# Decay rows of an attention tile: two transfers of 64 partitions in place of one with two source rows

## The chip, the cores and the metric

The kernel runs on one core of a Trainium2 chip. The metric is the device time of one execution in microseconds. A core has five engines with instruction streams of their own: PE (matrix multiply), DVE (vector), ACT (scalar, activation functions), POOL (general purpose) and SP, which here only issues transfers. Transfers are carried out by 16 DMA engines. Each engine runs its own stream in order and waits at semaphores for the others.

## The reference, cut to what matters

Three layers follow one another: a linear attention with decay, an MLP with x times cos(x), and a gated MLP. The change touches the attention.

```python
# x: (4, 8, 768, 32), a: (4, 8, 768), B and C: (4, 8, 768, 16); chunk = 32
for c in range(nc):
    la = log_a[:, :, sl]
    cum = np.cumsum(la, axis=-1)
    L = np.exp(cum[:, :, :, None] - cum[:, :, None, :]) * causal
    M = np.einsum('bhin,bhjn->bhij', Cc, Bc) * L
    y_intra = np.einsum('bhij,bhjd->bhid', M, xc)
    y_inter = np.einsum('bhin,bhnd->bhid', Cc, state) * np.exp(cum)[..., None]
    y[:, :, sl] = y_intra + y_inter
    Bx = np.einsum('bhjn,bhjd->bhjnd', Bc, xc) * decay_from_j[..., None, None]
    state = decay_full[..., None, None] * state + np.sum(Bx, axis=2)
x = y.transpose(0, 2, 1, 3).reshape(3072, 256)
h = x @ w_in                          # 256 -> 2048
x = (h * np.cos(h)) @ w_out           # 2048 -> 256
out = (sigmoid(x @ w_gate) * (x @ w_val)) @ w_out2   # 256 -> 1536 -> 256
```

## The kernel before

The 768 positions are cut into six blocks of 128 (`j`), and each block holds the four batches (`b`), so that a block of one batch is an attention tile: 128 tokens, eight heads. For `j` = 0 the tile is computed as one chunk of 128 (`add_att_first`). For `j` = 1 to 5 (`add_att`) it is two chunks of 64 tokens, and chunks and heads are laid over the partitions: partitions 0 to 63 hold one half of the heads, 64 to 127 the other.

The products of decays inside a chunk are made by one scan on the DVE (line 762): it runs over 512 columns (two chunks, four heads, 64 tokens) and writes the tile `lt`. Every partition needs the decays of all 64 tokens of its half of the heads, so the 512 values of a half are repeated over 64 partitions. This is the spread (`add_spread`, line 573): a transfer from `a_chunk`, a copy of the decays in DRAM, to a tile `ab` of 128 x 512 float32. There are three `ab` tiles in turn, and 20 spreads, one for each tile of blocks 1 to 5. Two products with `lt` follow: `bd` (line 765), which PE turns into the state's gain, and `g` (line 800), from which PE makes the tokens' output.

Beside the spread, `add_loads` (line 542) issues for every block: B and C (tile `bc`, 64 KB for each batch, 64-byte pieces), x (`xs`, 128 KB for each batch), two transfers that exchange the halves of x (`xw`), four that halve B (`bh`), and one for the decays of the state (`an`, from `a_clip`). The weights of the MLPs come as float64 words into slots of the tile `x2` (lines 354 and 359 for the first layer, 467 for the second), and ACT and DVE unpack them (lines 371 to 387): the step `three` on ACT (line 377) reads each load first. All transfers are issued by SP, in one order.

No order of instructions is written by hand. `Order.add` notes each step with its cost in nanoseconds for each engine that could do it, what it reads and what it writes. `Order.rank` gives it a due time, counted back from those who need it, and `Order.run` simulates the engines and always takes the step that can begin first, the more urgent one of two. For a step on SP the cost is the time that the transfer takes of a DMA pipe that all share, and `Issues(cost, n)` says that the step issues `n` transfers: SP is then held for 620 ns times `n`, or until the pipe has come to within 1100 ns of the transfer's end. A changed cost or number thus moves steps on every engine. MLP steps of the first layer begin as soon as the first block's attention and the first weights are there, and the planner interleaves them with the attention of later blocks.

Of the kernel before, what the change touches and what calls it, by code (L numbers as in the profile page):

```python
# [67 lines left out]
class Order:  # L68
# [17 lines left out]
    def add(self, where, fn, r=(), w=(), tag=None, turn=None):  # L86
        op = Op()
        op.engs, op.fn, op.tag, op.turn = dict(where), fn, tag, turn
        op.users, op.ready = [], {e: 0.0 for e in op.engs}
        deps = set()  # L90
        for x in r:
            if x in self.last_w:
                deps.add(self.last_w[x])
        for x in w:
            if x in self.last_w:
                deps.add(self.last_w[x])
            deps.update(self.reads.get(x, ()))
        i = len(self.ops)
        for x in r:
            self.reads.setdefault(x, []).append(i)  # L100
        for x in w:
            self.last_w[x] = i
            self.reads[x] = []
        op.left = len(deps)
        for d in deps:
            self.ops[d].users.append(i)
        self.ops.append(op)
# [111 lines left out]
def linear_attention__then__cos_mlp__then__gated_mlp_kernel(  # L219
# [23 lines left out]
    nc = tc.nc  # L243
    NB, H, S, D = x.shape
# [11 lines left out]
    add = order.add  # L256
# [8 lines left out]
    def ring(pool_, n, shape, dt, name):  # L265
        return [pool_.tile(shape, dt, name=f"{name}{i}") for i in range(n)]
# [37 lines left out]
    TC = T // 2  # L304
    a_chunk = dram.tile([NB, 2, 2 * NJ, 4, TC], F32, name="a_chunk")
# [4 lines left out]
    ab_t = ring(att_p, 3, [128, H * TC], F32, "ab")  # L310
# [231 lines left out]
    def add_loads(j):  # L542
        i = j % NL
        t = slice(j * T, (j + 1) * T)
        for b in range(NB):
            for src, dst, room, cost in ((C, bc_t[i][:, 1, b], ("bc", i, 1, b), 704), (B, bc_t[i][:, 0, b], ("bc", i, 0, b), 704),
                                         (x, x_whole(i, b), ("xs", i, b), 832)):
                add({"SP": cost}, lambda e, src=src, dst=dst, b=b: nc.sync.dma_start(  # L548
                    out=dst, in_=src[b, :, t, :].rearrange("h t n -> t h n")), w=[room])
        if j == 0:  # L550
            return

        def turn_x(e):
            for half in range(2):
                nc.sync.dma_start(
                    out=xw_t[i][HALF[half]],
                    in_=xs_t[i][HALF[1 - half]].rearrange("t (b g d) -> t b g d", b=NB, g=2)[:, :, half])

        def halve_b(e):
            for half in range(2):  # L560
                for c in range(2):
                    nc.sync.dma_start(  # L562
                        out=bh_t[i][HALF[half], c],
                        in_=bc_t[i][HALF[c], 0].rearrange("t b (g k) n -> t b g (k n)", g=2)[:, :, half])

        add({"SP": Issues(960, 2)}, turn_x, r=[("xs", i, b) for b in range(NB)], w=[("xw", i)])
        add({"SP": Issues(1536, 4)}, halve_b, r=[("bc", i, 0, b) for b in range(NB)], w=[("bh", i)])
        add({"SP": 800}, lambda e: nc.sync.dma_start(
            out=an_t[i].rearrange("p b t -> p (b t)"),
            in_=a_clip[:, j].rearrange("h b t -> h (b t)")[:, None].to_broadcast([H, N, NB * T])),  # L570
            r=[("a_clip", b) for b in range(NB)], w=[("an", i)])

    def add_spread(j, b):
        u = (j * NB + b) % 3
        add({"SP": 800}, lambda e: nc.sync.dma_start(
            out=ab_t[u],
            in_=a_chunk[b, :, 2 * j:2 * j + 2].rearrange("g c k t -> g (c k t)")[:, None].to_broadcast([2, TC, H * TC])),
            r=[("a_chunk", k) for k in range(4)], w=[("ab", u)] + (["a_f", "a_part", "a_res", "sel_b"] if u == 2 else []))

    def x_whole(i, b):  # L580
        return xs_t[i].rearrange("t (b h d) -> t b h d", b=NB, h=H)[:, b]

    HALF = (slice(0, 64), slice(64, 128))
# [510 lines left out]
    def open_later(e):  # L1094
# [18 lines left out]
        out=mask_sb[:, 0:64], in0=mask_sb[:, 0:64], in1=mask_sb[:, 64:128], op=ALU.add), w=["mask"])  # L1113
    add({"DVE": dve2(2)}, lambda e: nc.vector.tensor_copy(out=pair_sb, in_=mask_sb[:, 0:64:32]), r=["mask"], w=["pair"])
    for i in range(1, 4):
        add({"DVE": dve2(128), "POOL": pool(128)},
            lambda e, i=i: engine[e].tensor_copy(out=id4[:, i], in_=id_sb), r=["id"], w=["id4"])
    add_clip()
    add_loads(0)
    for b in range(NB):  # L1120
        add_att_first(b)
    add({"POOL": pool(512)}, lambda e: nc.gpsimd.tensor_tensor(
        out=id8, in0=id_sb[:, None, 0:TC].to_broadcast([128, H, TC]),
# [8 lines left out]
    for s, step in enumerate(steps):  # L1132
        j, f = step[:2]
        if j and f == 0:
            add_loads(j)
            for b in range(NB):
                add_spread(j, b)
                add_att(j, b)
        add_mlp1(s)
# [54 lines left out]
```

## Time and profile before

| | |
|---|---|
| median of 3 runs | 677.08 us (677.05 to 677.61) |
| the profiled execution | 676.78 us |
| its span, first to last instruction | 674.6 us |
| PE busy | 616.0 us (91%) |
| DVE, ACT, POOL busy | 509.2, 392.7, 195.0 us |
| mean granted PE clock | 0.971 of full speed |
| moved by transfers | 40.80 MB in 118552 packets |

The span is what the trace shows; 2.2 us of the profiled execution lie around it. Times in the trace count from the start of the span. Busy time tells how long an engine worked, not whether anybody waited for it; for that there are the waits (an instruction's idle time before it, and who ended it) and the chain that ended last.

### The profile page before, as it was taken

To read this page: it belongs to the slowest core of one execution; us is meant where nothing else is said; L and a number is where in the kernel's file an instruction comes from. 1 tells how busy PE (TensorE), PEld (TensorE's weight loads), DVE (VectorE), ACT (ScalarE), POOL (GpSimd) and SP (SyncE) were. 2 spreads that over 40 slices of the span, in tenths; PEclk is the share of its full clock that TensorE was granted. 3 is DMA by queue.
4 is the path that set the end of the run, shared out by engine and by line. 5 is a ranking of instruction groups with operands and counts; after the bars stand their busy time and mean duration, and the time that the engine had idled before them with its cause. 6 is when DMAs were issued, how large, how long until landed. Compare 5 with 4: busy or idle time off the path is not lost.

```text
span 674.6 us, 11328 instructions
## 1 busy us (share of the span) xinstructions
PE 616.0 (91%) x4260; PEld 490.7 (73%) x4260; DVE 509.2 (75%) x902; ACT 392.7 (58%) x672; POOL 195.0 (29%) x165
## 2 busy tenths in 40 slices
PE   4665696999969899999999999999999999999997
PEld 2343375787757678778678877888878888888886
DVE  7845684899847885886668889999997778775565
ACT  2324476876646567567578985776653346444442
POOL 2100234565325334335446743232100002010000
PEclk9995987999989999999999999999999999999999
DMA  6874749424352430000022122130002100021001
GB/s 121 131 189 112 148 81 206 94 60 82 76 137 67 123 83 1 28 7 1 2 64 78 48 63 63 62 95 0 1 5 35 26 0 1 1 35 29 1 1 62
DMA packets 118552, 40.80 MB, mean 60 GB/s; under 512 B 100387, under 2 KB 105539, under 8 KB 118499
## 3 DMA queue, kind: packets, MB, share of 16 engines
q1 hardware_dynamic: 118499, 40.09, 26.3%
q8 instruction: 33, 0.54, 0.4%
q14 instruction: 20, 0.16, 0.1%
HBM read 32.54 MB, written 4.92 MB: 56 GB/s over the span
## 4 chain that ended last, share of the span: by engine, by line
PE 73%; DMA 9%; SPq 7%; DVE 6%; ACT 2%; issue 2%; ACTq 0%; DVEq 0%
PE bank L328 62%; PE two_banks L328 10%; DMA x<-in_moe_w_out_dram 5%; SPq L548 4%; DMA ab<-a_chunk 2%; DMA bc<-in_C_dram 1%; DVE bank L1050 1%; SPq L562 1%; DVE gm L858 1%; SPq L354 1%; ACT gm L856 1%; DVE lt L762 1%; PE two_banks L747 0%; ACT gh L335 0%; DVE gm L854 0%
## 5 line engine op out<-in xcount | busy, mean ns | idle before, releaser
L340 POOL TENSOR_TENSOR gl<-gm,gh 128x512 fp32r<-128x512 f32 x104 | 148.3, 1429 | 315.2 <-ACT gh L335 200.3
L328 PE MATMUL bank<-xt_hi,w 128*128 128x512 f32 x573 | 161.5, 402 | 6.1 <-DVE gm L858 5.1
L328 PEld LDWEIGHTS bank<-xt_hi,w 128*128 128x128 f32 x573 | 108.5, 193 | 29.7 <-DVE gm L858 5.5
L1050 DVE TENSOR_TENSOR bank<-bank,cp 128x512 f32<-128x512 f32 x144 | 96.2, 694 | 43.4 <-PE bank L328 38.6
L328 PE MATMUL bank<-gh,w 128*128 128x512 f32 x408 | 116.0, 404 | 11.5 <-ACT gh L335 11.5
L335 ACT ACTIVATE gh<-gm 128x512 fp32r<-128x512 f32 x140 | 87.0, 627 | 60.7 <-DVE gm L1078 40.2
L328 PE MATMUL bank<-xt_lo,w 128*128 128x512 f32 x354 | 105.2, 395 | 0.0
L328 PEld LDWEIGHTS bank<-gh,w 128*128 128x128 f32 x408 | 78.2, 195 | 28.6 <-ACT gh L335 12.6
L858 DVE TENSOR_TENSOR gm<-gm,bank 128x512 f32<-128x512 f32 x96 | 65.2, 681 | 37.1 <-ACT gm L856 37.1
L852 ACT ACTIVATE gm<-bank,quarter_sb 128x512 int32<-128x512 f32 x96 | 65.2, 681 | 28.6 <-PE bank L328 22.4
L854 DVE TENSOR_TENSOR gm<-gm,bank 128x512 f32<-128x512 int32 x96 | 65.3, 682 | 21.9 <-ACT gm L852 21.2
L856 ACT ACTIVATE gm<-gm,right_sb 128x512 f32<-128x512 f32 x96 | 68.7, 718 | 19.2 <-DVE gm L854 18.3
L328 PEld LDWEIGHTS bank<-xt_lo,w 128*128 128x128 f32 x354 | 67.1, 191 | 14.1
L328 PE MATMUL bank<-gl,w 128*128 128x512 f32 x204 | 67.3, 405 | 0.2 <-POOL gl L340 0.2
L1075 ACT ACTIVATE gm<-bank 128x512 f32<-128x512 f32 x72 | 42.5, 599 | 41.7 <-DVE bank L1050 25.8
L335 ACT ACTIVATE cp<-bank 128x512 f32<-128x512 f32 x72 | 42.5, 597 | 29.0 <-PE bank L328 27.2
L1078 DVE TENSOR_TENSOR gm<-gm,bank 128x512 f32<-128x512 f32 x72 | 47.2, 681 | 2.2 <-PE bank L328 1.9
L328 PEld LDWEIGHTS bank<-gl,w 128*128 128x128 f32 x204 | 38.7, 195 | 8.5 <-POOL gl L340 0.6
L328 PE MATMUL bank<-xt_hi,own 128*128 128x512 f32 x135 | 37.7, 393 | 1.0 <-DVE bank L1050 1.0
L328 PE MATMUL bank<-op,w 128*128 128x512 f32 x126 | 34.9, 390 | 0.0
L328 PE MATMUL bank<-xt_lo,own 128*128 128x512 f32 x126 | 34.6, 390 | 0.2 <-ACT gm L1075 0.2
L340 DVE TENSOR_TENSOR gl<-gm,gh 128x512 fp32r<-128x512 f32 x46 | 31.2, 688 | 2.2 <-PE two_banks L328 1.4
(163 smaller groups left out, 838.4 us busy)
## 6 DMA issues: line engine op xcount, KB each, us to landing
x<-in_moe_w_out_dram SPq DMA_DIRECT2D x12, 512.0 KB
ab<-a_chunk SPq DMA_DIRECT2D x20, 256.0 KB
xs<-in_x_dram SPq DMA_DIRECT2D x24, 128.0 KB
x<-in_moe_w_in_dram SPq DMA_DIRECT2D x6, 512.0 KB
x<-in_moe_w_gate_dram SPq DMA_DIRECT2D x6, 512.0 KB
x<-in_moe_w_val_dram SPq DMA_DIRECT2D x6, 512.0 KB
out_dram<-x SPq DMA_DIRECT2D x128, 16.0 KB
bc<-in_C_dram SPq DMA_DIRECT2D x24, 64.0 KB
```

The source lines that it names most:

```text
L328: nc.tensor.matmul(out_, lhsT, rhs, start=start, stop=stop, skip_group_check=True)
L335: nc.scalar.activation(out=out_, in_=in_, func=ACTF.Copy)
L340: engine[eng].tensor_tensor(out=out_, in0=in0, in1=in1, op=ALU.subtract)
L354: nc.sync.dma_start(out=raw()[:, 0:256 * m].rearrange("p (k f) -> p k f", k=KD), in_=w_in[:, cols].rearrange("(k p) f -> p k f", p=128))
L548: add({"SP": cost}, lambda e, src=src, dst=dst, b=b: nc.sync.dma_start(out=dst, in_=src[b, :, t, :].rearrange("h t n -> t h n")), w=[room])
L852: add({"ACT": act_b(512) - 40}, lambda e: nc.scalar.activation(out=ri, in_=hp, func=ACTF.Identity, bias=quarter_sb), r=hr + ["round"], w=[ ...
L854: add({"DVE": dve(512)}, lambda e: nc.vector.tensor_tensor(out=g, in0=ri, in1=hp, op=ALU.subtract), r=hr, w=[("gm", u)])
L856: add({"ACT": act_b(512)}, lambda e: nc.scalar.activation(out=g, in_=g, func=ACTF.Sin, scale=-TURN, bias=right_sb), w=[("gm", u)])
L858: add({"DVE": dve(512)}, lambda e: nc.vector.tensor_tensor(out=g, in0=g, in1=hp, op=ALU.mult), r=hr, w=[("gm", u)])
L1050: add({"DVE": dve(512)}, lambda e: nc.vector.tensor_tensor(out=bank[to], in0=bank[x], in1=later["cp"][i], op=ALU.add), r=bank_r[x][:1] + [ ...
L1075: add({"ACT": act(512)}, lambda e, i=i, bk=bk: nc.scalar.activation(out=g_of("gm", i), in_=bank[bk], func=ACTF.Sigmoid), r=bank_r[bk][:1] ...
L1078: add({"DVE": dve(512)}, lambda e, i=i, bk=bk: nc.vector.tensor_tensor(out=g_of("gm", i), in0=g_of("gm", i), in1=bank[bk], op=ALU.mult), r ...
```

## The change

`add_spread` issues two transfers, one for each half of the partitions: 64 partitions, each of which reads the same 512 values. Before, one transfer went over 128 partitions, with a source of two rows, each repeated 64 times. The planner's cost of a spread stays 800 ns in all, and it is told that the step has two issues. The cost that the planner has for the transfer `an` is 1600 instead of 800 ns; that transfer itself is as it was.

```diff
@@ -565,16 +565,21 @@
-        add({"SP": 800}, lambda e: nc.sync.dma_start(
+        add({"SP": 1600}, lambda e: nc.sync.dma_start(
             out=an_t[i].rearrange("p b t -> p (b t)"),
             in_=a_clip[:, j].rearrange("h b t -> h (b t)")[:, None].to_broadcast([H, N, NB * T])),
             r=[("a_clip", b) for b in range(NB)], w=[("an", i)])
 
     def add_spread(j, b):
         u = (j * NB + b) % 3
-        add({"SP": 800}, lambda e: nc.sync.dma_start(
-            out=ab_t[u],
-            in_=a_chunk[b, :, 2 * j:2 * j + 2].rearrange("g c k t -> g (c k t)")[:, None].to_broadcast([2, TC, H * TC])),
+
+        def spread(e):
+            for half in range(2):
+                nc.sync.dma_start(
+                    out=ab_t[u][HALF[half]],
+                    in_=a_chunk[b, half, 2 * j:2 * j + 2].rearrange("c k t -> (c k t)")[None].to_broadcast([TC, H * TC]))
+
+        add({"SP": Issues(800, 2)}, spread,
             r=[("a_chunk", k) for k in range(4)], w=[("ab", u)] + (["a_f", "a_part", "a_res", "sel_b"] if u == 2 else []))
```

On SP, in the loads of block 2 (`bc_103`, `xs_101`) while block 1 is computed, the difference of the orders is this; `x_81` is the tile with the weights' slots, the numbers at the ends of names are those of buffers:

```order
 L548 DMA bc_103<-in_B_dram 128x8x16 x4
-L548 DMA xs_101<-in_x_dram 128x8x32 x4
-L575 DMA ab_107<-a_chunk 128x1x512
+L548 DMA xs_101<-in_x_dram 128x8x32 x3
 L354 DMA x_81<-in_moe_w_in_dram 128x2x256
 L359 DMA x_81<-in_moe_w_out_dram 128x2x256
+L548 DMA xs_101<-in_x_dram 128x8x32
+L578 DMA ab_107<-a_chunk 64x512 x2
 L562 DMA bh_115<-bc_103 64x4x64 x4
```

One pair of weight loads goes ahead of the last x load and of the spread of block 1's last tile.

On SP again, at the spreads of block 2's second and third tile and the loads of block 3 (`bc_104`, `xs_102`):

```order
+L578 DMA ab_105<-a_chunk 64x512 x2
 L548 DMA bc_103<-in_C_dram 128x8x16
-L575 DMA ab_106<-a_chunk 128x1x512
+L578 DMA ab_106<-a_chunk 64x512 x2
+L354 DMA x_81<-in_moe_w_in_dram 128x2x256
+L359 DMA x_81<-in_moe_w_out_dram 128x2x256
 L548 DMA bc_103<-in_C_dram 128x8x16 x2
 L548 DMA bc_104<-in_B_dram 128x8x16 x4
+L548 DMA xs_102<-in_x_dram 128x8x32 x4
+L562 DMA bh_116<-bc_104 64x4x64 x4
 L354 DMA x_81<-in_moe_w_in_dram 128x2x256
 L359 DMA x_81<-in_moe_w_out_dram 128x2x256
```

The pair that came after two C loads and four B loads comes before them, right behind the spread, and the next pair takes its place.

## Rows read from the trace of the kernel before

**Rows 1.** The page, busy us (share of the span) xinstructions of the PE.

```profile
PE 616.0 (91%) x4260; PEld 490.7 (73%) x4260; DVE 509.2 (75%) x902; ACT 392.7 (58%) x672; POOL 195.0 (29%) x165
```

**Rows 2.** Busy time by stretch; the first line names the columns.

```profile
core 0: us, PE busy (x) PEld busy (x) DVE busy (x) ACT busy (x) POOL busy (x), PEclk, DMA share, GB/s
0.00:26.00 26.00, 14.20 (x112) 8.30 (x112) 19.50 (x46) 7.83 (x19) 5.12 (x10) 1.00 0.77 130
...
26.00:127.00 101.00, 69.50 (x583) 49.49 (x576) 64.05 (x106) 52.43 (x86) 24.85 (x18) 0.85 0.70 147
...
100.00:126.00 26.00, 20.34 (x80) 16.18 (x78) 14.19 (x20) 16.76 (x25) 10.74 (x7) 0.87 0.95 185
...
160.00:200.00 40.00, 34.12 (x351) 26.39 (x352) 29.63 (x67) 21.05 (x40) 13.92 (x12) 0.98 0.49 111
```

**Rows 3.** The chain that ended last: start us, us, what.

```profile
38.23 11.87 DMA ab<-a_chunk
...
54.90 10.07 DMA bc<-in_C_dram
...
72.85 10.10 DMA x<-in_moe_w_out_dram
...
185.74 2.67 DMA xs<-in_x_dram
...
189.85 7.08 DMA x<-in_moe_w_out_dram
```

**Rows 4.** Busy time by stretch, columns as above: spreads alone, and xw alone.

```profile
51.00:57.00 6.00, 1.71 (x32) 1.14 (x32) 3.03 (x7) 4.30 (x7) 0.67 (x1) 0.54 0.13 50
...
251.00:252.20 1.20, 1.20 (x7) 1.00 (x6) 1.04 (x3) 1.20 (x4) 0.08 (x1) 1.00 0.84 176
```

**Rows 5.** Issues: KB of each; ns min/median/max of the issue, first and last start.

```profile
ab<-a_chunk SPq DMA_DIRECT2D x20, 256.0 KB
...
L575 SPq DMA_DIRECT2D ab<-a_chunk x20: 488/541/5282, 27.3 to 281.2; - x20
...
L555 SPq DMA_DIRECT2D xw<-xs x10: 590/622/2322, 36.2 to 250.5; - x10
```

**Rows 6.** Instructions of SP in order of time: start us, us, what.

```profile
27.26 0.58 SPq L575 DMA_DIRECT2D ab<-a_chunk  x1
...
49.57 5.28 SPq L575 DMA_DIRECT2D ab<-a_chunk  x1
...
85.38 3.99 SPq L575 DMA_DIRECT2D ab<-a_chunk  x1
```

**Rows 7.** Instructions of PE and ACT: start, us, what [idle before it, who ended it].

```profile
35.49 1.08 PE L328 MATMUL two_banks<-g,xs 128*32 128x128 f32 x16 [2.23 <-DMA xs<-in_x_dram]
...
50.34 0.33 PE L747 MATMUL two_banks<-id_t,bc 128*128 128x128 f32 x1 [3.58 <-DMA bc<-in_C_dram]
...
52.79 0.32 PE L328 MATMUL bank<-xs,bd 64*32 64x64 f32 x2 [2.12 <-DVE bd L765]
...
58.47 0.47 PE L747 MATMUL bank<-id_t,bc 128*128 128x128 f32 x1 [3.97 <-DMA bc<-in_C_dram]
...
65.01 0.47 PE L747 MATMUL two_banks<-id_t,bc 128*128 128x128 f32 x1 [1.24 <-DMA bc<-in_C_dram]
...
83.04 1.19 ACT L377 ACTIVATE x<-x,low_sb 128x1024 int32<-128x1024 uint32 x1 [7.16 <-DMA x<-in_moe_w_out_dram]
...
85.61 2.07 PE L328 MATMUL bank<-xt_hi,w 128*128 128x512 f32 x4 [5.15 <-DVE gm L858]
...
107.71 2.07 PE L328 MATMUL bank<-gh,w 128*128 128x512 f32 x4 [5.66 <-ACT gh L335]
...
199.46 2.08 PE L328 MATMUL bank<-gh,w 128*128 128x512 f32 x4 [5.88 <-ACT gh L335]
```

**Rows 8.** Busy time by stretch, columns as in rows 2: behind that wait.

```profile
198.20:205.00 6.80, 5.54 (x13) 4.39 (x14) 4.58 (x7) 5.39 (x10) 3.82 (x3) 0.50 0.02 6
```

**Rows 9.** Waits of SP's queue from 130 to 420 us: us, times, longest.

```profile
SPq L575 <- DVE lt L762: 31.6, 7, 6.9
```

## Prediction

> **What bounds the kernel now.** The first view is the page's busy times [rows 1]: the PE works for 616.0 of 674.6 us, so 58.6 us of PE idleness is all that a change of transfers can win, apart from clock. The second is the table of stretches [rows 2], to see where that idleness lies. From 26 to 127 us the PE is busy for 69.50 of 101.00 us, and the DMA engines for a share of 0.70. This is the stage in which the first blocks' inputs and the first layer's weights arrive; more than half of the idleness, 31.5 us, is there. The third is the chain that ended last [rows 3]. In this stage it runs through transfers: a spread at 38.23 that took 11.87 us, a C load that took 10.07, a weight load that took 10.10. These are 256 KB, 64 KB and 512 KB; times this long for so little are queueing, so I ask for what.
>
> From 51 to 57 us spreads alone were moving [rows 4]: the DMA share is 0.13 and the rate 50 GB/s. A share of 0.13 of 16 engines is 2.1 engines. So one spread runs on two engines, as many as it has source rows, and its 256 KB (262,144 bytes) [rows 5] take 262/50 = 5.2 us. The other 14 engines are free meanwhile, but not for what comes behind: a transfer that uses all 16 has a piece on each, and lands when its pieces on the two busy ones have had their turn. The SP too is held: at 49.57 and 85.38 us the issue of a spread took 5.28 and 3.99 us instead of a median of 541 ns [rows 5, 6].
>
> Seven of the 20 spreads are issued in the stage, the first at 27.26 and the last at 85.38 us [rows 6]. Its DMA work is 0.70 x 101 = 70.7 us per engine. The spreads are 7 x 5.2 = 36.7 us on two engines, 36.7 x 2/16 = 4.6 as a mean over 16, so everything else is 66.1. If that is evenly laid, the two engines have 66.1 + 36.7 = 102.8 us to do in 101: they are full from end to end, and they set the stage. It fits that the PE's waits there are for what queued behind spreads [rows 7]: x 2.23 us, C 3.58, 3.97 and 1.24, the decay product that follows the scan of a spread 2.12, and 5.15 and 5.66 for MLP results that stand on ACT behind the unpacking of a weight load; at 83.04 us ACT had waited 7.16 us for one [rows 7]. Together that is 24.0 of the 31.5 us.
>
> **The change, part by part.** *The transfer.* Two transfers of 64 partitions and 64 source rows replace one. The nearest row is the pair that turns x (xw, also 64 partitions and 128 KB each): from 251.0 to 252.2 us it ran at 0.84 of 16 engines and 176 GB/s [rows 4]. So I expect each half on all 16. At 176 GB/s a pair takes 262/176 = 1.5 us, which at a share of 0.84 is 1.25 us of each engine. The other end is the spread's own rate on eight times the engines, 5.24/8 = 0.66. Seven cost 4.6 to 8.8 us; I take the middle, 6.7, since nothing here shows 16 engines reading one row. The two full engines come down from 102.8 to 66.1 + 6.7 = 72.8 us, as all others.
>
> *What the stage then takes.* Queues are never full all the time. The share was 0.77 from 0 to 26 us, where no spread runs, and 0.95 from 100 to 126 us, where the spreads are through [rows 2]. With the middle, 0.86, the stage takes 72.8/0.86 = 84.7 us, 16.3 less. The ends are 70.7/0.95 = 74.4 (26.6 less) and 74.9/0.77 = 97.3 (3.7 less). The compute engines can follow: 69.50 us of PE work and 64.05 of DVE work [rows 2] are 82% and 76% of 84.7. The mean granted clock of the stage is only 0.85 of full speed [rows 2], but I add nothing for it: the stage is set by DMA.
>
> *Later.* From 127 us the PE is nearly full but for 160 to 200 us, where 5.9 us are idle [rows 2]. They are the wait of 5.88 us at 199.46 [rows 7], and the chain gives its reason: an x transfer waited for until 188.4, then a weight load that took 7.08 us [rows 3]. After it the granted clock was 0.50 from 198.20 to 205.00 us, with 5.54 us of PE work in it [rows 8], which at the full clock would be 2.8 shorter. So 0 to 8.7 us are to be had. I take 4.0, a little under half, because here the SP also waits for the scans to free a buffer, 31.6 us in seven waits [rows 9], and these stay.
>
> *The SP.* An issue with 64 partitions took 622 ns (xw), one spread 541 [rows 5]. Two are 0.70 us more each time, 7 x 0.70 = 4.9 us in the stage. What covers this are the two blocked issues, 5.28 + 3.99 - 2 x 0.54 = 8.2 us, that should go. Without that cover the 4.9 us would be lost. The 13 later ones, 9.1 us, lie beside the waits for scans.
>
> *The order.* The planner is told of one more issue per spread and of 1600 instead of 800 ns for the decay transfer an. It answers by pulling weight loads ahead of x loads and of the fourth block's B and C loads. That is to the good for the two longest PE waits (85.61 and 107.71 us), which hang on weights. It costs nothing on its own as long as the staging buffer is free when SP comes to the load; otherwise x, B and C queue behind a waiting SP. No instruction is added on PE, DVE, ACT or POOL. I count it as nothing, inside the stage.
>
> Sum: 16.3 + 4.0 = 20.3 us. The profiled execution took 676.78 us, 0.3 less than the median of the runs, 677.08. So 676.8 - 20.3 = 656.5 us, and 656.8 for the median. The bounds are 26.6 + 8.7 = 35.3 (641.8) and 3.7 + 0 (673.4).
>
> **The rivals.** *A new wait takes the place.* In-order engines find the next late thing: DVE at 76% has little slack, ACT stands behind each unpacking, SP behind a staging buffer. Of the seven PE waits all 24 us would have to shrink; if only those on C and x do (2.23 + 3.58 + 3.97 + 1.24 = 11.0) and half of that comes back as another wait, the gain is 5.5 and the time 672. Chance 0.13.
>
> *The split gives nothing.* The Trainium skill (DMA: Bandwidth & Descriptors, Rules for kernel authors) says of two transfers to disjoint partition halves "Don't bother": both spray over the same 16 engines and serialize. By that rule the 4.9 us of issues are all that changes, which is 682. The rows speak against it here, because the single transfer was on 2.1 engines, not 16 [rows 4]; another section of that page (Why a DMA increments its semaphore by 16 and not by 1) takes the engine count from the outermost sizes of both sides, which would be 2 before, as the trace has it, and 16 now, which no run here shows for a repeated row. Chance 0.04.
>
> *One hot source row.* This one ends slower. All 64 descriptors of a half read the same 2 KB, now from 16 engines at once. Two engines on a row each got 25 GB/s per row [rows 4]. If a row gives no more than that to all its readers, a half takes 5.2 us and a pair 10.5, on all 16 engines: 66.1 + 7 x 10.5 = 139.6 us instead of 102.8, some 37 us longer, 714. It decides from the point where a pair takes over 5.2 us, below 50 GB/s. For it: nothing shows several engines on one row. Against it: two rows at 25 GB/s each are at one engine's pace, so the engine and not the row was the limit. Chance 0.05.
>
> *It does not do what it says.* The repeated row may be laid on one or two engines again: two halves at 2.6 us on two engines or in turn, the stage as before, 677. Chance 0.05.
>
> **How the numbers follow.** The forecast has 0.73, of which some 0.04 lie below its lower bound; with the new wait 0.86 are faster. Same 0.05. Slower are the split that gives nothing and the hot row, 0.09. The range 642 to 673 holds the forecast and the new wait; left out are 0.14 on the slow side and the 0.04 below. A measurement of this kernel tells 0.2%, 1.4 us, from no change.
>
> **What would show it.** Where only spreads move, the DMA share must be near 0.8 and not 0.13; no issue of a spread over 1.5 us; the stretch with the first weights must end near 111 us instead of 127; C loads in the chain of 2 to 4 us instead of 10; the PE's waits for C gone, the 5.88 us near 199 us shorter. The prediction is wrong if the share while spreads move stays at 0.13 (not wide), if it is high but the rate under 50 GB/s (hot row), or if DMA is idle in the stage while DVE or ACT is waited for (new wait).

## The result and the profile after

The changed kernel takes 640.06 us (median of 4 runs, 638.3 to 641.48) against 677.35 us in the same comparison: a ratio of 0.9445, 95% interval 0.9417 to 0.9473, some 37 us less. The forecast was 656.8 us, its range 642 to 673. The sign and the mechanism were right, the size was not: the gain is nearly twice the one forecast, and the time lies 2 us below the range.

The profiled execution of the changed kernel took 641.48 us, with a span of 639.7. The page's busy times, as in [rows 1]:

```profile
PE 609.3 (95%) x4260; PEld 486.6 (76%) x4260; DVE 505.9 (79%) x901; ACT 392.2 (61%) x674; POOL 191.8 (30%) x164
```

The PE's idleness is 639.7 - 609.3 = 30.4 us, where it was 58.6. Busy time by stretch, with the columns of [rows 2]:

```profile
26.00:101.00 75.00, 66.03 (x586) 47.92 (x582) 63.14 (x107) 51.42 (x85) 24.74 (x17) 0.85 0.97 187
...
76.00:91.00 15.00, 15.00 (x68) 12.30 (x67) 12.83 (x19) 13.64 (x21) 8.01 (x6) 1.00 1.04 174
...
116.10:117.90 1.80, 1.80 (x10) 1.49 (x9) 1.77 (x5) 1.76 (x4) 0.96 (x2) 1.00 0.50 139
122.00:124.00 2.00, 2.00 (x11) 1.65 (x10) 2.00 (x7) 1.66 (x4) 0.08 (x2) 1.00 0.56 131
...
160.00:200.00 40.00, 38.06 (x383) 29.36 (x383) 32.60 (x60) 26.78 (x49) 16.86 (x13) 0.99 0.47 122
```

The first line is the stage that took from 26 to 127 us before [rows 2]. It now ends near 101, and the DMA share in it is 0.97 where it was 0.70. The second line is a part of that stage: the PE is busy throughout, and the share reads 1.04. A share over 1 means that the times of packets overlap, so it does not tell by itself that the engines can do no more. The third and the fourth line are stretches in which one spread moves alone. Before, such a stretch had a share of 0.13 [rows 4]; now a spread costs 0.50 x 1.80 = 0.90 us (for 139 x 1.80 = 250 of its 262 KB, so 0.94 for the whole) or 0.56 x 2.00 = 1.12 us, as a mean over 16 engines. The last line is the late place: of 40 us the PE idles for 1.9, where it idled for 5.9 [rows 2].

Two stretches of matmuls that stand in the chain of either kernel, in the same place of the work, show where the time went. In the chain of the kernel before (start us, us, what):

```profile
135.04 17.62 PE bank L328 x92
...
242.19 28.16 PE bank L328 x124
```

In the chain of the changed kernel, with the longest waits for transfers ahead of them:

```profile
35.05 8.09 DMA an<-a_clip
...
43.15 7.15 DMA bc<-in_C_dram
...
74.33 5.36 DMA x<-in_moe_w_out_dram
...
93.69 5.88 DMA x<-in_moe_w_out_dram
...
108.25 17.62 PE bank L328 x92
...
207.11 28.14 PE bank L328 x124
```

The first mark comes 26.8 us earlier and the second 35.1. So 26.8 us were won up to the end of the first stage, 8.3 us between the marks, and nothing behind them: the span is 34.9 us shorter. (This execution is the slowest of the four, 1.4 us above their median, and has the lowest mean granted clock of them, 0.976 against 0.990 to 0.995; its trace shows 35 of the 37 us. A mark is read from one execution. The kernel of "The late gain" below does the same work up to the first mark and came there at 106.21 us instead of 108.25, so differences of marks are good to some 2 us.)

The PE's waits for what queued behind spreads have gone or shrunk. This is the only wait of 1 us or more that the PE has between 45 and 128 us, in the form of [rows 7]:

```profile
50.43 0.45 PE L752 MATMUL bank<-id_t,bc 128*128 128x128 f32 x1 [1.88 <-DMA bc<-in_C_dram]
```

The waits of 5.15 and 5.66 us for MLP results have no counterpart here, and that of 5.88 us near 199 has none later: from 100 to 240 us the longest wait of the PE is 1.65 us.

### The profile page after: what moved, and what is told of

It reads as the page before. It is cut to its first block, busy times and chain, and to the rows that moved or that the text cites. A ratio compares the mean times of both kernels' runs of the same rounds, so it can differ in the third digit from the quotient of the medians.

```text
span 639.7 us, 11356 instructions
## 1 busy us (share of the span) xinstructions
PE 609.3 (95%) x4260; PEld 486.6 (76%) x4260; DVE 505.9 (79%) x901; ACT 392.2 (61%) x674; POOL 191.8 (30%) x164
## 2 busy tenths in 40 slices
DMA packets 119152, 40.80 MB, mean 64 GB/s; under 512 B 100987, under 2 KB 106139, under 8 KB 119099
## 4 chain that ended last, share of the span: by engine, by line
PE 75%; DVE 10%; DMA 6%; ACT 5%; issue 2%; SPq 1%; DVEq 0%; ACTq 0%
PE bank L328 63%; PE two_banks L328 11%; DMA x<-in_moe_w_out_dram 3%; DVE bank L1055 1%; DMA an<-a_clip 1%; DMA bc<-in_C_dram 1%; DVE gm L863 1%; DVE lt L767 1%; ACT gh L335 1%; DVE gm L859 1%; ACT stk L648 1%; DVE g L805 1%; DVE w L340 1%; DMA ab<-in_a_dram 1%; SPq L562 1%
## 5 line engine op out<-in xcount | busy, mean ns | idle before, releaser
L340 POOL TENSOR_TENSOR gl<-gm,gh 128x512 fp32r<-128x512 f32 x104 | 146.6, 1413 | 282.6 <-ACT gh L335 187.2
L328 PE MATMUL bank<-gh,w 128*128 128x512 f32 x408 | 113.4, 397 | 0.0
L861 ACT ACTIVATE gm<-gm,right_sb 128x512 f32<-128x512 f32 x96 | 68.7, 719 | 21.1 <-DVE gm L859 20.2
L328 PE MATMUL bank<-gl,w 128*128 128x512 f32 x204 | 65.9, 398 | 0.2 <-POOL gl L340 0.2
L328 PEld LDWEIGHTS bank<-gl,w 128*128 128x128 f32 x204 | 37.3, 190 | 8.7 <-POOL gl L340 1.6
L328 PE MATMUL bank<-xt_hi,own 128*128 128x512 f32 x135 | 37.7, 392 | 1.0 <-DVE bank L1055 1.0
L328 PE MATMUL bank<-op,w 128*128 128x512 f32 x126 | 34.9, 390 | 0.0
L340 DVE TENSOR_TENSOR gl<-gm,gh 128x512 fp32r<-128x512 f32 x46 | 31.1, 688 | 1.9 <-PE two_banks L328 1.4
```

The lines of the kernel that those rows point to most:

```text
L328: nc.tensor.matmul(out_, lhsT, rhs, start=start, stop=stop, skip_group_check=True)
L340: engine[eng].tensor_tensor(out=out_, in0=in0, in1=in1, op=ALU.subtract)
L861: add({"ACT": act_b(512)}, lambda e: nc.scalar.activation(out=g, in_=g, func=ACTF.Sin, scale=-TURN, bias=right_sb), w=[("gm", u)])
```

## The experiments

The theory was that a spread sits on as many DMA engines as it has source rows, and that what is queued behind it waits for these. Times are medians; each ratio is to the kernel before in the same comparison, with its 95% interval.

### The order alone, and the split alone

The new steps and costs, with the old transfer in `spread`:

```diff
         def spread(e):
-            for half in range(2):
-                nc.sync.dma_start(
-                    out=ab_t[u][HALF[half]],
-                    in_=a_chunk[b, half, 2 * j:2 * j + 2].rearrange("c k t -> (c k t)")[None].to_broadcast([TC, H * TC]))
+            nc.sync.dma_start(
+                out=ab_t[u],
+                in_=a_chunk[b, :, 2 * j:2 * j + 2].rearrange("g c k t -> g (c k t)")[:, None].to_broadcast([2, TC, H * TC]))
```

> The new order of all queues, but each spread as one transfer with two source rows, as before. Theory 1 (what counts is that a spread sits on two DMA engines and holds up what is queued behind it there): no gain, 670 to 684 us. Rival 2 (the new order, with weight loads ahead of x, B and C loads, brings a third or more of the 37 us): at most 664 us.

And the two transfers with the planner's old numbers, so with the old order:

```diff
-        add({"SP": 1600}, lambda e: nc.sync.dma_start(
+        add({"SP": 800}, lambda e: nc.sync.dma_start(
...
-        add({"SP": Issues(800, 2)}, spread,
+        add({"SP": 800}, spread,
```

> The order of before, but each spread as two transfers of 64 partitions. Theory 1: nearly the whole gain, 639 to 648 us. Rival 2 (the order brings a third or more): 652 us or more.

Measured: the order alone 669.93 us, 0.9907 (0.987 to 0.9944); the split alone 645.53 us, 0.9536 (0.95 to 0.9573). Of 677 us these are 6.3 and 31.4 us, and their sum, 37.7, is the gain of both, 37.6. So the split is the larger part by far, and its time is in the range that the theory gave. But the order is worth six us by itself, which no theory had: its 669.93 lies 0.07 us below the 670 to 684 of "no gain" and far from a third. With the split it is worth as much: 0.9536 - 0.9445 is 6.2 us, and the two intervals do not touch. The same two marks of the chain, for the order alone:

```profile
130.81 17.62 PE bank L328 x92
...
235.96 28.16 PE bank L328 x124
```

and for the split alone:

```profile
113.60 17.62 PE bank L328 x92
...
211.48 28.16 PE bank L328 x124
```

The split alone brings 21.4 us to the first mark and 9.3 us between the marks. The order adds 5.3 us up to the first mark (113.60 to 108.25); the 1.0 us that it costs between them is less than marks tell. What it does is seen on SP: with the split alone the last weight load of the first layer is issued at 101.45 us, behind two C loads, four B loads and one more C load (91.84 to 100.77 us); in the changed kernel it is issued at 93.69, and seven such loads come behind it (94.20 to 101.94 us). The issue with the split alone:

```profile
101.45 0.46 SPq L359 DMA_DIRECT2D x<-in_moe_w_out_dram  x1
```

### How many engines: two transfers on two, and two on four

Two transfers for each spread, but cut by columns, so that each still has two source rows:

```diff
-            for half in range(2):
+            for c in range(2):
                 nc.sync.dma_start(
-                    out=ab_t[u][HALF[half]],
-                    in_=a_chunk[b, half, 2 * j:2 * j + 2].rearrange("c k t -> (c k t)")[None].to_broadcast([TC, H * TC]))
+                    out=ab_t[u][:, c * 256:(c + 1) * 256],
+                    in_=a_chunk[b, :, 2 * j + c].rearrange("g k t -> g (k t)")[:, None].to_broadcast([2, TC, 256]))
```

> Two transfers for each spread, in the new order, but cut by columns: 128 partitions and 256 columns each, so each still has two source rows. Theory 1: still two engines, a DMA share of 0.13 while spreads move alone, 675 to 692 us. Rival 3 (two transfers in flight in place of one are what helps, or a shorter wait of the SP at each issue): 640 to 655 us.

And halves whose source has four rows:

```diff
-                    in_=a_chunk[b, half, 2 * j:2 * j + 2].rearrange("c k t -> (c k t)")[None].to_broadcast([TC, H * TC]))
+                    in_=a_chunk[b, half, 0:8].rearrange("(r c) k t -> r (c k t)", r=4)[:, None].to_broadcast([4, 16, H * TC]))
```

> Two transfers of 64 partitions as in the change, but the source of each has four rows of 2 KB, each repeated 16 times (the rows are not the tile's own, so the decays are wrong; the work is the same). Theory 1: four engines, 2.6 us of each for a spread, so these four have 66.1 + 7 x 2.6 = 84.3 us in the first stage instead of about 72.8: the stage is 10 to 14 us longer than in the changed kernel, and the time 646 to 660 us. Rival 4 (any widening frees the SP, and the length on the engines does not matter): 638 to 643 us.

Measured: by columns 678.99 us, 1.0033 (1.002 to 1.0047); with four rows 648.02 us, 0.9585 (0.9557 to 0.9612). The DMA share where spreads move nearly alone, by columns:

```profile
56.00:60.00 4.00, 0.03 (x1) 0.06 (x2) 2.85 (x7) 1.23 (x2) 1.27 (x1) 0.50 0.14 44
```

and with four rows:

```profile
123.00:125.00 2.00, 2.00 (x11) 1.65 (x10) 1.95 (x5) 1.93 (x4) 1.15 (x1) 1.00 0.23 87
```

A share of 0.14 is 2.2 engines and 0.23 is 3.7. So the engines go by source rows and not by transfers: two transfers that stay on two engines bring nothing, and even cost 0.3% beside the 6 us that the order should have given. Their pieces are half as long, 1 KB, and move at 44 GB/s instead of 50 [rows 4]; for seven spreads that is 7 x (262/44 - 262/50) = 5.0 us more, an estimate that would take up most of the order's gain. Four engines have most of the gain. Nor is it SP that was freed: with four rows the issues of the stage's seven spreads take SP 13.8 us, more than the 12.5 of the kernel before, and the gain is there all the same. (By columns they take 21.1 us, so that run alone would not part the engines from SP.) Theory 1 holds, rivals 3 and 4 fall. The dose is smaller than worked out, though: the load that follows the stage (the first of the gate's weights) goes out at 108.77 us instead of 101.98, 6.8 us later and not 10 to 14 (the first mark, 115.13 against 108.25, says the same).

The pages' packet counts show the number of engines in another way. Packets of under 512 bytes number 100387 in the kernel before, 100427 by columns, 100507 with four rows, 100667 with one transfer from a single row (below), 100987 in the changed kernel and 101627 with four transfers (below). Over 20 spreads the excess is 2, 6, 14, 30 and 62 packets each. In the trace's packet records these are packets of 4 bytes beside a spread's data, 2 for each spread before and 32 in the changed kernel. Where the share gives two and four engines, that is one for each engine of each transfer: 2 before, 2 x 2 by columns, 2 x 4 with four rows. By the same count the others are 1 x 16, 2 x 16 and 4 x 16. So the single repeated row is laid over 16 engines, although the share of a spread alone is only 0.50.

### Is SP on the path, and are the engines full?

One transfer of 128 partitions from one repeated row:

```diff
-            for half in range(2):
-                nc.sync.dma_start(
-                    out=ab_t[u][HALF[half]],
-                    in_=a_chunk[b, half, 2 * j:2 * j + 2].rearrange("c k t -> (c k t)")[None].to_broadcast([TC, H * TC]))
+            nc.sync.dma_start(
+                out=ab_t[u],
+                in_=a_chunk[b, 0, 2 * j:2 * j + 2].rearrange("c k t -> (c k t)")[None].to_broadcast([128, H * TC]))
```

> The changed kernel's order, but each spread as one transfer of 128 partitions whose source is a single row repeated 128 times (the second half gets the first half's decays; the work is the same but for 20 issues less). Theory 1 (the 16 DMA engines are now the bound of the first stage, and SP's issues are covered): as the changed kernel, 637 to 642 us. Rival 5 (the second issue of each pair is now on the path): 20 x 0.58 = 11.6 us less, of which 4 or more show, at most 635 us. Rival 6 (many readers of one row slow each other down): 646 us or more.

Four transfers of 32 partitions:

```diff
-            for half in range(2):
+            for p in range(4):
                 nc.sync.dma_start(
-                    out=ab_t[u][HALF[half]],
-                    in_=a_chunk[b, half, 2 * j:2 * j + 2].rearrange("c k t -> (c k t)")[None].to_broadcast([TC, H * TC]))
+                    out=ab_t[u][32 * p:32 * p + 32],
+                    in_=a_chunk[b, p // 2, 2 * j:2 * j + 2].rearrange("c k t -> (c k t)")[None].to_broadcast([32, H * TC]))
```

> The changed kernel's order, each spread as four transfers of 32 partitions: the same bytes on the same number of engines, 40 issues of 0.58 us more, 14 of them in the first stage (8.1 us of SP). Theory 1: covered, 639 to 645 us. Rival 5 (SP's issues are on the path): 648 us or more.

The pair issued twice, first to a place that nobody reads:

```diff
+    extra = dram.tile([NJ * NB, 128, 512], F32, name="extra")
...
         def spread(e):
+            for half in range(2):
+                nc.sync.dma_start(
+                    out=extra[j * NB + b, HALF[half]],
+                    in_=a_chunk[b, half, 2 * j:2 * j + 2].rearrange("c k t -> (c k t)")[None].to_broadcast([TC, H * TC]))
             for half in range(2):
```

> The changed kernel with every pair issued twice, the first time to a place in DRAM that nobody reads: as many issues as with four transfers (641.3 us), but twice the spread bytes on the 16 engines. Theory 1 (in the first stage the DMA engines' own time is the bound): seven more pairs of about 0.9 us on each engine, 645 to 650 us. Rival 9 (the engines have slack in the stage, and DVE, ACT or PE is the bound): at most 643 us.

Measured: one transfer 636.44 us, 0.9408 (0.9384 to 0.9432); four 641.33 us, 0.9477 (0.9455 to 0.9499); doubled 643.03 us, 0.9525 (0.9503 to 0.9547). One transfer and four each overlap the changed kernel's interval, one from below and one from above. The issues of one transfer, ns min/median/max:

```profile
L577 SPq DMA_DIRECT2D ab<-a_chunk x20: 319/339/2411, 27.1 to 240.3; - x20
```

of two, in the changed kernel:

```profile
L578 SPq DMA_DIRECT2D ab<-a_chunk x40: 444/582/1225, 27.3 to 246.6; - x40
```

and of four:

```profile
L578 SPq DMA_DIRECT2D ab<-a_chunk x80: 302/419/1384, 27.5 to 248.2; - x80
```

By the medians a spread thus holds SP for 0.34, 1.16 or 1.68 us, and the three times rise in that order, 636.4, 640.1 and 641.3; only the first and the last are clear of each other. The engines' work is nearly the same in the three: by the pages' shares of the main queue, times the span, 187.6, 188.1 and 188.9 us for each engine in the whole run. So SP's issues do not seem to be wholly covered, as theory 1 had it, nor are they the bound: one transfer lies between the 637 us of theory 1 and the 635 that rival 5 asked for. Since the step from two to four was only 0.52 us for a spread and not the 1.16 of the expectation, this run tells less than it was made for. Rival 6 falls: 128 readers of one row are no slower.

The doubled kernel's 643.03 us lie below theory 1's 645 to 650 and at the bound of rival 9, but the kernel before was faster in that comparison, 675.24 us; by its ratio the time would be 645.2 beside 677.35. Its ratio is 0.0080 above the changed kernel's, 5.4 us, and 0.0048 above that of four transfers, 3.2 us; its interval is clear of both, of the latter barely. An extra pair, which goes to DRAM, costs less than was expected: the page's share of the main queue is 31.1% of 642.6 us, 199.8 us for each engine, where the changed kernel has 188.1, so 0.6 us for each of 20 pairs and some 4 us for seven. Most of that shows, so the engines' time counts. That it alone ends the stage is not shown: the extra pairs bring as many issues with them, and the PE too is full for much of the stage, 15.00 of 15.00 us from 76 us on in the table above.

### The late gain

The two transfers in blocks 1 and 2, the old one in blocks 3 to 5:

```diff
         def spread(e):
+            if j > 2:
+                nc.sync.dma_start(
+                    out=ab_t[u],
+                    in_=a_chunk[b, :, 2 * j:2 * j + 2].rearrange("g c k t -> g (c k t)")[:, None].to_broadcast([2, TC, H * TC]))
+                return
             for half in range(2):
```

> The changed kernel's order; the spreads of blocks 1 and 2 as two transfers, those of blocks 3 to 5 as one with two source rows. Theory 1 with its late term (the idle 5.9 us and the half clock near 199 us of the kernel before come from spreads too): the late gain of 8 to 9 us goes and the early one stays, 646 to 652 us. Rival 7 (the late gain follows from the early one, since everything is due earlier): 638 to 643 us.

Measured: 647.63 us, 0.9578 (0.9544 to 0.9611), 0.0133 or 9.0 us above the changed kernel. The late wait is back, in the PE's timeline of this kernel:

```profile
169.93 2.07 PE L328 MATMUL bank<-gh,w 128*128 128x512 f32 x4 [5.19 <-ACT gh L335]
```

and its chain shows the same cause as in [rows 3], between the same two marks:

```profile
106.21 17.62 PE bank L328 x92
...
160.35 7.05 DMA x<-in_moe_w_out_dram
...
213.17 28.16 PE bank L328 x124
```

From the first mark to the second it takes 106.96 us, the kernel before 107.15, the changed kernel 98.86. So theory 1's late term stands: the late loss was made by the spreads of the later blocks, and rival 7 falls. With the order alone, and the old spreads all through, the second mark came 6.2 us earlier than before and the first 4.2; whether the 2.0 us between them are the order's is not shown, since marks tell no more than that.

### Which of the planner's two numbers

The split with one of the two numbers put back, first the cost of `an`, then the told second issue:

```diff
-        add({"SP": 1600}, lambda e: nc.sync.dma_start(
+        add({"SP": 800}, lambda e: nc.sync.dma_start(
```

> Split spreads, the planner told of two issues each, but an at 800 as before. Part of the weight loads of the second shown place stand later again, behind two C loads and a B load. Theory 8 (the order's 5 us come from that place, where one pair of weight loads goes ahead of the C and B loads): most of them go, 643 to 647 us. Rival 8 (they come from the first place, or from the told second issue): 638 to 642 us.

```diff
-        add({"SP": Issues(800, 2)}, spread,
+        add({"SP": 800}, spread,
```

> Split spreads, an at 1600, but the planner told of one issue for each spread. The weight loads stand behind two C loads and two B loads. Theory 8: 643 to 647 us. Rival 8 (the price of an is what counts): 638 to 642 us.

Measured: 641.96 us, 0.9503 (0.9469 to 0.9537), and 641.21 us, 0.9494 (0.9466 to 0.9521). As times both lie in rival 8's range, but the kernel before was at 675.24 us in that comparison; by the ratios they would be 643.7 and 643.1 beside 677.35, in theory 8's. Both lie between the split alone and the changed kernel and overlap with each. Nothing is told apart; which place of the order brings its us stays open.

### Two attempts at a faster kernel

`a_clip` written twice, so that `an` has 16 source rows:

```diff
-    a_clip = dram.tile([H, NJ, NB, T], F32, name="a_clip")
+    a_clip = dram.tile([H, 2, NJ, NB, T], F32, name="a_clip")
...
-            in_=a_clip[:, j].rearrange("h b t -> h (b t)")[:, None].to_broadcast([H, N, NB * T])),
+            in_=a_clip[:, :, j].rearrange("h r b t -> (h r) (b t)")[:, None].to_broadcast([2 * H, N // 2, NB * T])),
...
         for b in range(NB):
+            for r in range(2):
...
```

> The changed kernel, with the decays of the state (a_clip) written twice to DRAM, so that the transfer an has 16 source rows of eight repeats in place of eight of sixteen, at the price of four more small issues at the start. Theory 1 (engine time is the bound of the first stage): three an transfers of about 2 us on eight engines become 1 us on sixteen, 637 to 640 us. Rival (the four issues, 2.3 us, delay the start and nothing comes back): 641 to 643 us.

`a_chunk` copied eight times, so that one transfer has 16 source rows with the right decays:

```diff
+        add({"SP": 3000}, lambda e: nc.sync.dma_start(
+            out=a_rep, in_=a_chunk.rearrange("b g c k t -> (b g) (c k t)")[:, None].to_broadcast([2 * NB, 8, 2 * NJ * 4 * TC])),
+            r=[("a_chunk", k) for k in range(4)], w=["a_rep"])
...
+            nc.sync.dma_start(
+                out=ab_t[u],
+                in_=a_rep[2 * b:2 * b + 2].rearrange("g r x -> (g r) x")[:, None, o:o + H * TC].to_broadcast([16, 8, H * TC]))
```

> The changed kernel with one transfer for each spread and the right decays: a_chunk is first copied eight times to DRAM by one transfer, so a spread of 128 partitions has 16 source rows of eight repeats. Theory 1: 16 engines again, 20 issues less, one copy of 768 KB more at the start: 636 to 641 us. Rival (the copy delays the first spread or the first weights): 642 us or more.

Measured: 638.82 us, 0.944 (0.9421 to 0.946), which can't be told from the changed kernel, and 643.88 us, 0.9529 (0.9504 to 0.9554), 5.7 us slower than it. Its first spread is issued at 31.10 us instead of 27.29, as the rival had it; but the planner also counts one issue for a spread and 3000 ns for the copy, so its order is another, and what each costs is not told apart. No kernel that computes the whole was shown to be faster than the changed one.

## Why the prediction was right and wrong

**Right: what a spread does.** "One spread runs on two engines, as many as it has source rows" was read from a share of 0.13; shares of 0.14 for two rows in two transfers and 0.23 for four rows confirm it, and the packet counts do. Its price on 16 engines was put at 0.95 us (6.7/7) and is 0.94 or 1.12. The work of the stage was put at 72.8 us on each engine; 0.97 x 75 is 72.8 us, but so close a match is luck, since the stretches do not hold the same transfers: 147 x 101 us is 14.8 MB before, 187 x 75 is 14.0 after. The issues were to stay under 1.5 us, and the longest took 1.225.

**Signs that did not come as named.** The share of a spread alone is 0.50 or 0.56 and not near 0.8. The stage ends near 101 us and not 111. The C load in the chain took 7.15 us and not 2 to 4, and the PE still waits 1.88 us for it. Ahead of it in the chain stands `an`, with 8.09 us. Its source has eight rows, so it is a transfer of the same kind; with 16 rows for it the kernel was not told apart from the changed one (above).

**Wrong: the step "with the middle, 0.86, the stage takes 72.8/0.86 = 84.7 us".** The share is 0.97, above even the upper end of 0.95, and the stage takes 75 us. Nor was it a filling that one may divide by: it reads 1.04 from 76 to 91 us. The middle was taken with the stretch from 0 to 26 us, which had no spread, but also no full queue: that it was fit to stand for the stage was never argued. The stretch from 100 to 126 us, with 0.95, was a stretch of this stage with the spreads through, and was the nearer row: 72.8/0.95 is 76.6 us. On the marks, the split alone gives 21.4 us where this term said 16.3: 5.1 us of the miss.

**Wrong: "the order ... I count it as nothing, inside the stage".** It is worth 6.3 us without the split and 6.2 with it, 5.3 of them up to the first mark. The text itself named the two waits that the pulled weight loads would shorten; it gave them no us because the stage was taken to end when the engines have done all their work, in which no order could matter. But in the chain the stage ends with the last weight load (93.69 us, 5.88 us long), and the order sets how much is issued ahead of it: seven C and B loads that stood ahead of it with the split alone come behind it in the changed kernel.

**Wrong in size: "I take 4.0" for the later part.** It was 8.3 us on the marks, near the upper bound of 8.7. The halving was argued from SP's waits for scans, which do stay:

```profile
SPq L578 <- DVE lt L767: 36.1, 9, 5.8
```

That is even more than the 31.6 us of [rows 9], and the late loss is gone all the same. So these waits were not what made the weights late.

So of the 35.1 us on the second mark 20.3 were forecast, and 5.1 for the share, 5.4 for the order and 4.3 for the later part are missing, each read from single executions and good to some 2 us. The upper bounds of the first and the third gave 641.8 us in the text. The order was given neither a value nor a bound, and with it the time could pass that end, as it did.

**The rivals.** A new wait of the old size did not come: DVE works 63.14 of 75 us in the stage, 84%, and the PE 66.03, 88%. The hot row did not come either: 0.94 or 1.12 us for a spread, where 5.2 would have turned the sign. That the repeated row might not be laid wide is refuted by the packet counts. For the split that gives nothing there was the rule of the Trainium skill (DMA: Bandwidth & Descriptors, Rules for kernel authors) that two transfers to disjoint partition halves serialize and should be one. Here the trace differs: the split alone brought 31 us, because the one transfer had not been on all 16 engines. Where it is, the rule's advice agrees with the runs: one transfer of 128 partitions from a single row took 636.44 us, no longer than the pair. Whether the two halves serialize, no run here was made to show.

## What to carry to other kernels

When transfers that follow a repeated load land late, look at the DMA share of a stretch in which that load moves alone. The share times 16 was 2.1 for two engines and 3.7 for four; for 16 it was only 8 or 9, so take it as the least number of engines, and compare packet counts. Here a load on two of 16 engines held up the wider transfers behind it on the same queue: a C load of 64 KB took 10.07 us [rows 3]. Add up what the fullest engines have to do, not the mean: here the mean share was 0.70, and by the prediction's sum the two had 102.8 us of work in 101. For a stage that a resource will bound after the change, take its share from that stage's own full stretches, and remember that it can read more than 1. And ask what stands ahead of the awaited load in the order of issues.

## What was not expected of the hardware

The time that SP is held by one issue depends on the form: a median of 339 ns for 128 partitions from a single repeated row, 541 ns for 128 partitions from two rows [rows 5], 582 ns for 64 partitions from one, 419 ns for 32. So one wide transfer was issued in less time than any of the narrower ones. A spread costs 0.94 or 1.12 us as a mean over 16 engines, against 0.66 if 16 engines each had kept the pace of the two; whether it is the one row or the number of engines that costs the difference, no run here parts.
